# The second MLP product of two more chunks by seven block products, and a new order for every engine

## The chip, the cores and the metric

The kernel runs on one core of a Trainium2 chip. The core has five engines, each with a queue of its own that it works off in order: PE (TensorE, matrix products), DVE (VectorE), ACT (ScalarE), POOL (GpSimd) and SP (SyncE, here only issuing DMAs). DMAs are also issued from the queues of POOL and ACT. An instruction that waits holds up everything behind it in its queue. The metric is the device time of one execution in microseconds (us).

## The reference

Two stages follow each other. The first is attention over 4 batches, 8 heads, 768 positions and 64 features, in which a query sees the 8 first keys and the 96 last ones:

```python
scores = scale * np.matmul(q, k.transpose(0, 1, 3, 2)) + bias
a = softmax(np.where(is_global | is_local, scores, -1e9))
x = np.matmul(a, v)                      # heads side by side: 4 x 768 x 512
```

The second takes the real part of a two-dimensional Fourier transform of x, adds x, normalises and applies an MLP of width 2048:

```python
u = x + np.real(fft(fft(x, axis=1), axis=2))
un = (u - mean(u)) / np.sqrt(var(u) + 1e-6)
out = u + np.maximum(un @ w_ch1, 0.0) @ w_ch2
```

## The kernel before

**Stages.** The four batches go one after the other through attention (functions `trans`, `score`, `av`), the transform (`fold_0` for batch 0 and `fold_s`, `fold_d` for the others on DVE, `y_unit` and `u_unit` on PE) and the MLP. The work of different batches overlaps: while the MLP of one batch fills PE, the attention and transform of the next are put between its products. The MLP works on 12 chunks of 256 rows, three to a batch, each made of two tiles of 128 rows.

**First product.** `ph_unit(c, jp)` makes two of the 16 blocks of 128 hidden features of chunk c: eight matmuls of 256 columns into a bank `ph` (there are two such banks), then the ReLU on ACT (line 1383) or DVE (line 1384) into the tile `hT` of the chunk. Two chunks' hidden values have a place at a time, so chunk 2 can start when chunk 0's second product is done. Chunks 9 to 11 make the first product by seven block products (class `Seven`, line 1471), which is not touched.

**Second product, plain form.** Chunks 0 and 1 (all c below `CS = 2`) use `pg_unit`: for each of the two row tiles, four parts of four matmuls of 512 columns (line 1583), each part needing one quarter of W2 and two `ph` units. DVE then takes the bank, multiplies by the reciprocal deviation of the row (made on POOL, lines 1329 and 1330, token `rstd`) and adds u (line 1594); a DMA stores the result.

**Second product, seven block products.** The other chunks use `s_sums` and `pg_units`. The hidden values of a chunk are four blocks A(t, half), by row tile and by half of the hidden features; W2 is four blocks B(half, column half). With sums of A blocks (S1 to S4, four DVE instructions of 128x1024, lines 1661 to 1674) and sums of B blocks (made once), seven products of a 128x1024 by a 1024x256 block do the work of eight. The units are p1, p45 (two products), p6, p7 and p32 (two products), on line 1697; each product is eight matmuls of 256 columns. After each unit DVE evicts the bank and adds to u (line 1715): 256 columns for p1 and p6, 512 for the others.

**Sums of W2.** `w2_sums(i)`, for the two halves i of the blocks, has two pieces: `one` (token `w2a`, line 1633) makes B11-B01 in the tile `misc`, which until then holds the tables of the masks for the scores of batches 0 and 1; `rest` (token `w2t`, lines 1637 to 1639) makes three more, one of them in place, over a block of W2 itself. As `pg_unit` reads that block, `rest` has to wait until the eight last parts of chunks 0 and 1 are done (token `pgdone`). Two of the sums lie in the tile `tt`, which holds queries and keys of batch 1 first and then the rows x of batch 1; `rest` waits for those to be read.

**Order.** A planner (class `Plan`) emits the instructions; the order on each engine is written out in `ORDER`, as a list of names for each of the five queues. A letter names the stream: A for attention, M for the transform ("mixing"), H for the first product, G for the second; `T` is everything made at set-up. `G4.0` is the first piece of other engines' work that follows PE unit `G4`. A name stands in the list of the engine that does it, so that the list also says whether ACT or DVE makes a ReLU or a copy. Before, G0 to G15 are the parts of chunks 0 and 1, and G16 to G20 are p1, p45, p6, p7 and p32 of chunk 2. The eight quarters of W1 and W2 are loaded by DMAs from POOL (lines 1888 and 1893).

Of the kernel before, what the change touches and what calls it, by code (L numbers as in the profile page):

```python
# [12 lines left out]
ALU = mybir.AluOpType  # L13
# [11 lines left out]
class Plan:  # L25
# [132 lines left out]
            if ring.n == 0:  # L158
                self.rings[ring].append((ring.e, ring.k))

    SHARED = {"kB": 1, "vB": 1, "sid": 1, "f1": 0, "f2": 0, "f3": 0, "z": 0, "g0": 0, "w": 0, "s": 0, "su": 0, "w2a": 0, "w2t": 0, "ex": 0}
    SLOW = ((0.56, 1.0, 1.0), (0.38, 0.7, 1.0))
    COPIES = ("vB", "kB")
    ports = ()
# [75 lines left out]
    def unit_start(self, unit):  # L240
# [7 lines left out]
        if not there:  # L248
# [11 lines left out]
    EARLY = ("qk2", "qk1", "v0", "v2", "qk3", "v1", "v3")  # L260
    ORDER = {
# [10 lines left out]
        ),  # L272
        "ACT": (
# [10 lines left out]
        ),  # L284
        "DVE": (
# [13 lines left out]
        ),  # L299
        "POOL": (  # L300
# [5 lines left out]
        ),  # L306
        "SP": (
            "T.6 T.0 T.9 T.127 T.35 T.133 T.10 T.128 G7.1 T.91 T.134 T.136 G3.1 T.137 T.130 T.100 T.131 T.101 T.176 T.182 T.102 T.177 T.185 T.34 T.206 "
            "T.183 T.140 T.186 T.212 T.205 T.211 T.179 T.149 T.180 T.263 T.150 T.151 T.222 T.223 T.228 T.189 T.229 T.198 T.199 T.200 T.245 T.239 T.240 "
            "T.246 T.258 T.256 T.257 "  # L310
        ),
    }

# [61 lines left out]
def dve2(n):  # L375
    return 0.075 + n / 1920.0
# [7 lines left out]
def kernel(  # L384
# [22 lines left out]
    FB = 2  # L407
    DM = ()
    PEF = (1, 3)
    CS = 2  # L410
    NTD = 3
    assert (B, H, S, Dh, NG, NL) == (4, 8, 768, 64, 8, 96)

# [1214 lines left out]
    def w2_sums(i):  # L1628
        k0 = slice(4 * i, 4 * i + 4)
        k1 = slice(NK + 4 * i, NK + 4 * i + 4)  # L1630

        def one():
            VT(W2T(1)[:, k0], W2[0][:, k1, HC:Dm], W2[0][:, k0, HC:Dm], op=ALU.subtract)

        def rest():
            w = W2[0]
            VT(W2T(3)[:, k0], w[:, k0, HC:Dm], w[:, k0, 0:HC], op=ALU.subtract)
            VT(W2T(0)[:, k0], w[:, k1, HC:Dm], W2T(3)[:, k0], op=ALU.subtract)
            VT(W2T(2)[:, k0], w[:, k1, 0:HC], W2T(0)[:, k0], op=ALU.subtract)
        pl.later([("DVE", dve2(1024), one)], [("w2", 3), ("w2", 1)] + [("ex", 1, hp, g) for hp in range(HP) for g in range(3)], 0.0, [("w2a", i)], rank=2)  # L1640
        pl.later([("DVE", 3 * dve2(1024), rest)], [("w2a", i), ("pgdone",)] + free("tt", WTI), 0.0, [("w2t", i)], rank=2)

    def s_sums(c):
        hs = [("h", c, jp) for jp in range(NJ // 2)]
# [43 lines left out]
    def pg_units(c):  # L1688
# [99 lines left out]

        h0 = [("h", c, jp) for jp in range(4)]
        h1 = [("h", c, jp) for jp in range(4, 8)]  # L1790
        ws = [("w2t", 0), ("w2t", 1)]
        wd = [("w2", a) for a in range(4)]
        PG.append((h0 + wd + [("D",)], ("pg", "ph") if c >= NP * B - 2 else ("pg",), p1))
        PG.append((h1 + [("s", c, 1)] + ws, ("pg", "ph") if c >= NP * B - 2 else ("pg",), p45))
        PG.append(([("s", c, 2), ("ra", c, 0)] + ws, None, p6))
        if lean:
            PG.append(([("s", c, 3), ("ra", c, 1), ("w2a", 0), ("w2a", 1)], None, p7))
# [213 lines left out]
```

## Time and profile before

| | |
|---|---|
| runs shown | 243.38, 244.39, 245.47 us; median 244.39 |
| profiled execution | 244.25 us, span of its instructions 242.4 us |
| granted TensorE clock | 1.000 |
| busy in the span: PE, weight loads | 230.6 us, 188.2 us |
| busy: DVE, ACT, POOL | 206.4, 143.3, 115.7 us |
| HBM read, written | 31.44 MB, 8.65 MB |

How to read the rows of the profile that follow: "L1697" is line 1697 of the kernel; a group's row has line, engine, operation, output <- input, the shape, the count, then "busy us, mean ns of one" and the idle time of the engine just before it. "PE pgD L1697 <- DVE tt L1639: 1.1, 1, 1.1" among the waits says that PE was idle 1.1 us in total, once, for 1.1 us at most, before line 1697, until DVE's line 1639 had written `tt`. A chain piece such as "59.23 1.73 PE pg L1583 x8" has start, length, engine, tile, line and count. In a row of a stretch of time ("24.20:50.20") stand its length, then the busy time of PE, of its weight loads (PEld), of DVE, ACT and POOL, each with its count of instructions, the granted clock, the DMA share and the GB/s.

### The profile page before, as it was taken

The page shows a single profiled execution, that of the slowest core. Times are in us where ns is not written, and L with a number is a line of the kernel's source. Part 1 is how long each engine was busy: PE and PEld are TensorE (multiplying, and loading weights), DVE is VectorE, ACT ScalarE, POOL GpSimd, SP SyncE. Part 2 cuts the span into 40 slices and gives each one's busy share as a digit, 9 for nine tenths or more (in the row PEclk, how much of TensorE's full clock was granted, in tenths as well). Part 3 has the DMA queues.
Part 4 walks back from the last instruction along what each step waited for, and adds up shares of the span by engine and source line. Part 5 has one row for each costly group of instructions (what it writes and reads, how often), then busy time and mean ns, then how long its engine had stood idle before and what let it go on. Part 6 is the DMA issues. An engine that isn't in the chain of part 4 may idle for free.

```text
span 242.4 us, 7226 instructions
## 1 busy us (share of the span) xinstructions
PE 230.6 (95%) x3026; PEld 188.2 (78%) x3026; DVE 206.4 (85%) x463; ACT 143.3 (59%) x233; POOL 115.7 (48%) x161
## 2 busy tenths in 40 slices
PE   7898899899999999889999999999999999999993
PEld 3465677598677668678988888898889899888882
DVE  3478997979961898999999899999998899988992
ACT  2288469974127978665268848845754588376300
POOL 8998769975800319999029854104140350003020
PEclk9999999999999999999999999999999999999999
DMA  7999999999999998999999956964892363103003
GB/s 181 166 164 180 203 209 193 206 207 168 129 159 178 206 182 66 136 178 96 133 220 294 200 76 192 177 32 87 252 271 46 78 141 66 25 0 143 34 26 147
DMA packets 103248, 35.44 MB, mean 146 GB/s; under 512 B 91088, under 2 KB 98640, under 8 KB 103216
## 3 DMA queue, kind: packets, MB, share of 16 engines
q0 software_dynamic: 72448, 19.16, 78.1%
q1 hardware_dynamic: 27216, 13.08, 25.6%
q10 hardware_dynamic: 3552, 2.75, 4.6%
q8 instruction: 23, 0.38, 0.6%
q14 instruction: 9, 0.07, 0.1%
HBM read 31.44 MB, written 8.65 MB: 165 GB/s over the span
## 4 chain that ended last, share of the span: by engine, by line
PE 77%; DVE 12%; ACT 4%; DMA 3%; issue 2%; POOL 1%; DVEq 0%; SPq 0%; POOLq 0%
PE ph L1378 22%; PE pgD L1697 14%; PE pgA L1697 10%; PE phA L1471 4%; PE py L1139 4%; PE pav L856 4%; PE pg L1583 4%; PE phX L1471 3%; DMA qkT<-qk 3%; ACT ex L800 3%; PE pu L1226 3%; PE pz L1860 2%; DVE x L868 2%; DVE ex L812 2%; PE sc L771 2%
## 5 line engine op out<-in xcount | busy, mean ns | idle before, releaser
L1378 PE MATMUL ph<-unT,w 128*128 128x256 f16 x576 | 71.4, 273 | 0.0
L1378 PEld LDWEIGHTS <-w 128*128 128x128 f16 x576 | 55.2, 98 | 8.4
L1383 ACT ACTIVATE hT<-ph 128x512 f16<-128x512 f32 x63 | 36.9, 596 | 41.7 <-PE ph L1378 41.4
L1697 PEld LDWEIGHTS <-hT 128*128 128x128 f16 x288 | 27.8, 98 | 4.8 <-issue 1.4
L797 ACT ACTIVATE er<-sc 128x1024 f16<-128x1024 f32 (+1 forms) x24 | 22.2, 951 | 10.0 <-DVE ex L812 6.0
L800 ACT ACTIVATE ex<-sc 128x1024 f16<-128x1024 f32 (+1 forms) x24 | 21.4, 959 | 8.5 <-PE sc L739 8.5
L1329 POOL TENSOR_SCALAR sm<-sm 128x2 f32<-128x2 f32 x12 | 5.2, 432 | 42.2 <-ACT un L1322 41.6
L1568 POOL DMA_INDIRECT out_dram<-u,back x4 | 5.4, 1345 | 30.7 <-DVE u L1715 30.4
L569 POOL DMA_DIRECT2D qk<-in_k_dram x16 | 13.5, 845 | 12.6 <-DMA qkT<-qk 8.4
L1715 DVE SCALAR_TENSOR_TENSOR u<-pgA,sm,u 128x256 f32<-128x256 f32 (+1 forms) x30 | 16.9, 565 | 1.5 <-PE pgA L1697 1.4
L1715 DVE SCALAR_TENSOR_TENSOR u<-pgD,sm,u 128x512 f32<-128x512 f32 (+1 forms) x21 | 15.0, 719 | 2.6 <-PE pgD L1697 2.5
L812 DVE TENSOR_TENSOR ex<-er,mk 128x1024 f16<-128x1024 f16 (+1 forms) x24 | 16.1, 688 | 0.0
L1583 PE MATMUL pg<-w,hT 128*128 128x512 f16 x64 | 15.5, 379 | 0.0
L1322 ACT ACTIVATE un<-un 128x512 f16<-128x512 f16 x24 | 15.0, 629 | 0.5 <-DMA unT<-un 0.5
L856 PE MATMUL pav<-v,ex 128*128 128x65 f16 x224 | 13.1, 193 | 1.9 <-DVE x L868 1.1
L856 PEld LDWEIGHTS <-ex 128*128 128x128 f16 x352 | 12.7, 97 | 2.8 <-issue 1.1
L569 POOL DMA_DIRECT2D qk<-in_q_dram x16 | 13.9, 879 | 0.0
L1152 ACT ACTIVATE zy<-py 128x1024 f16<-128x1024 f32 (+1 forms) x13 | 10.7, 825 | 4.3 <-PE py L1139 4.2
L868 DVE TENSOR_TENSOR x<-pav,rc 128x384 f16<-128x384 f32 x24 | 12.6, 554 | 0.6
L1384 DVE TENSOR_SCALAR hT<-ph 128x512 f16<-128x512 f32 x9 | 6.2, 685 | 7.1 <-PE ph L1378 7.0
L624 ACT ACTIVATE qk<-phA 128x512 f32<-128x512 f32 x12 | 6.9, 595 | 7.8 <-PE phA L1471 7.8
L1139 PE MATMUL py<-t,ww 128*128 128x256 f16 x80 | 11.2, 273 | 0.0
(217 smaller groups left out, 563.8 us busy)
## 6 DMA issues: line engine op xcount, KB each, us to landing
w<-in_moe_w_ch_dram POOLq DMA_DIRECT2D x8, 512.0 KB, 11.4
out_dram<-u SPq DMA_DIRECT2D x15, 256.0 KB, 3.5
v<-in_v_dram POOLq DMA_DIRECT2D x16, 192.0 KB, 7.0
qk<-in_k_dram POOLq DMA_DIRECT2D x16, 96.0 KB, 4.9
qk<-in_q_dram POOLq DMA_DIRECT2D x16, 96.0 KB, 5.0
xr<-xd SPq DMA_DIRECT2D x3, 512.0 KB, 4.0
xd<-x ACTq DMA_DIRECT2D x2, 768.0 KB, 5.3
ex<-w POOLq DMA_DIRECT2D x3, 512.0 KB, 6.7
```

Source lines behind the costliest of these rows:

```text
L569: nc.gpsimd.dma_start(qk16[n][:, w, :, h], src[b, h0 + h].rearrange("(i m) d -> m i d", m=P))
L797: A(mine(), cut(pa), AF.Exp, 0.0, 0.125)
L800: A(cut(expst[hp][:, :, g * 512:g * 512 + (384 if g == 2 else 512)]), cut(pa), AF.Exp, 0.0, 0.125)
L812: VT(o, mine(), m, op=ALU.mult)
L856: nc.tensor.matmul(o[:, s * 65:(s + 1) * 65], lhsT, w, start=(a == 0), stop=(a == len(ops) - 1), skip_group_check=True)
L868: VT(X[b][:, 3 * (k.start + h):3 * (k.start + h) + 3, 2 * hp * Dh:(2 * hp + 2) * Dh].rearrange("p y (h d) -> p y h d", d=Dh), pv[:, h, :, ...
L1139: nc.tensor.matmul(o, lhsT, rhs, start=(x == 0), stop=(x == len(ops) - 1))
L1378: nc.tensor.matmul(ph[:, a * CH:(a + 1) * CH].rearrange("p (x m) -> p x m", x=2), W1[0][:, d, jb * P:(jb + 1) * P], UNT[c][:, :, d, :], st ...
L1383: pl.later([("ACT", act(512), lambda: A(dst, ph, AF.Relu)), ("DVE", dve(512), lambda: V.tensor_scalar_max(dst, ph, 0.0))], [], e, [("h", c ...
L1583: nc.tensor.matmul(pg, HT[c][:, jb, t * P:(t + 1) * P], W2[0][:, jb, :], start=(jb == 0), stop=(jb == NJ - 1))
L1697: nc.tensor.matmul(o, lhs(j), rhs(j), start=(first and j == 0), stop=(j == NK - 1), skip_group_check=True)
L1715: V.scalar_tensor_tensor(o, x, r(t), acc, op0=ALU.mult, op1=ALU.add)
```

## The change

- `CS` goes from 2 to 0: chunks 0 and 1 also make their second product by `s_sums` and `pg_units`, and `pg_unit` is no longer used. No one waits for `pgdone`.
- With `CS = 0` the rows x of batch 1 lie where those of batch 0 lay (tile `x`) and no longer in `tt`; the sums of W2 in `tt` wait for the queries and keys only.
- `w2_sums` gets three pieces: `one` (one instruction), `middle` (two, token `w2b`) and `rest` (one, the sum in place). They make the same four sums in the same eight instructions. `one` of half i now names the two quarters of W2 that it reads (i and 2 + i) instead of quarters 1 and 3; p6 needs `middle`, p45 also `rest`.
- The lists of all five engines are new.

In the new lists G0 to G4 are p1, p45, p6, p7, p32 of chunk 0, G5 to G9 of chunk 1, and so on; T.270 to T.275 are the pieces of `w2_sums` (`one`, `middle`, `rest` of half 0, then of half 1); T.201 to T.204 and T.207 to T.210 are S1, S2, S4, S3 of chunks 0 and 1. Thirty pieces of work that DVE did go to ACT and one to POOL; eight that ACT did and four that POOL did go to DVE. Of these, in the stretch from about 24 to 50 us: the copies of the turned queries and keys of pairs 5 to 7 (`A26.1`, `A30.1`, `A34.1`), the copy of batch 0's rows `M5.0`, a scaling copy `M0.1`, the copy of chunk 0's turned rows `M10.0` and two evictions of the transform (`M3.0`, `M8.1`) go from DVE to ACT; four such evictions (`M0.0`, `M2.1`, `M3.1`, `M8.0`) go from ACT to DVE, and key copies `A25.0`, `A26.0`, `A30.0` from POOL to DVE.

The diff, with the lists cut to the parts of PE and DVE in which chunks 0 and 1 have their second product:

```diff
-    SHARED = {..., "w2a": 0, "w2t": 0, "ex": 0}
+    SHARED = {..., "w2a": 0, "w2b": 0, "w2t": 0, "ex": 0}
...
         "PE": (
...
-            "A28 M2 M3 M8 A39 A32 M7 A33 A31 A40 M6 A27 M9 M10 M12 A41 H2 H3 A44 H5 H4 A42 H1 A43 H6 M11 H0 H7 M13 G4 G0 H13 G5 G6 H9 H14 G1 G7 G2 H8 "
-            "M18 G3 H15 M15 H11 H10 G8 H16 H18 G12 H12 M14 H17 H20 A47 A46 G9 G13 M16 A51 G14 G10 H19 A53 H21 G11 A45 G15 M17 H23 H22 G16 H30 A52 A54 "
+            "A39 M3 A28 A32 M9 M7 A29 A40 M6 A27 M12 A33 A41 A31 M10 A43 H6 A42 H0 A44 H7 H3 M11 H4 H2 H1 H12 H15 H11 H5 H8 H10 G0 H14 H13 M13 G1 H9 G2 "
+            "M14 M15 G3 M18 G4 G5 H16 H19 A46 A47 H17 H20 A53 A51 G7 G6 A45 M16 G8 H21 H18 M17 H23 G10 H22 G9 A56 A54 H24 A57 H29 H31 A52 H26 G12 A48 "
...
         "DVE": (
...
-            "M7.11 M10.0 M7.12 M7.10 M12.0 M12.2 A41.0 M7.13 A44.0 A42.0 A43.0 M12.4 M12.5 T.93 H7.0 T.94 T.95 T.96 T.97 T.98 M13.0 H14.0 H15.0 G7.0 "
-            "G3.0 H12.0 M14.0 H17.0 T.123 T.261 T.259 A47.1 M16.0 H20.0 M16.2 A46.1 M16.6 A51.1 A53.1 G11.0 G15.0 T.260 T.201 T.262 A45.1 T.202 G16.0 "
+            "M12.0 M12.2 M7.11 A41.0 A43.0 T.273 A42.0 A44.0 T.274 T.93 T.275 T.94 T.95 T.270 T.96 T.271 T.272 T.201 T.97 T.202 G0.0 T.98 G2.0 T.204 "
+            "T.203 G1.0 G3.0 T.207 M18.0 T.208 G4.0 G5.0 A46.1 T.210 A47.1 H17.0 H20.0 G7.0 A53.1 A51.1 G6.0 M16.0 G8.0 M16.2 T.209 A45.1 M16.6 T.123 "
...
-    CS = 2
+    CS = 0
...
         def one():
             VT(W2T(1)[:, k0], W2[0][:, k1, HC:Dm], W2[0][:, k0, HC:Dm], op=ALU.subtract)
 
+        def middle():
+            VT(W2T(0)[:, k0], W2[0][:, k0, 0:HC], W2T(1)[:, k0], op=ALU.add)
+            VT(W2T(2)[:, k0], W2[0][:, k1, 0:HC], W2T(0)[:, k0], op=ALU.subtract)
+
         def rest():
-            w = W2[0]
-            VT(W2T(3)[:, k0], w[:, k0, HC:Dm], w[:, k0, 0:HC], op=ALU.subtract)
-            VT(W2T(0)[:, k0], w[:, k1, HC:Dm], W2T(3)[:, k0], op=ALU.subtract)
-            VT(W2T(2)[:, k0], w[:, k1, 0:HC], W2T(0)[:, k0], op=ALU.subtract)
-        pl.later([("DVE", dve2(1024), one)], [("w2", 3), ("w2", 1)] + [("ex", 1, hp, g) for hp in range(HP) for g in range(3)], 0.0, [("w2a", i)], rank=2)
-        pl.later([("DVE", 3 * dve2(1024), rest)], [("w2a", i), ("pgdone",)] + free("tt", WTI), 0.0, [("w2t", i)], rank=2)
+            VT(W2T(3)[:, k0], W2[0][:, k0, HC:Dm], W2[0][:, k0, 0:HC], op=ALU.subtract)
+        pl.later([("DVE", dve2(1024), one)], [("w2", i), ("w2", 2 + i)] + [("ex", 1, hp, g) for hp in range(HP) for g in range(3)], 0.0, [("w2a", i)], rank=2)
+        pl.later([("DVE", 2 * dve2(1024), middle)], [("w2a", i)] + free("tt", WTI), 0.0, [("w2b", i)], rank=2)
+        pl.later([("DVE", dve2(1024), rest)], [("w2a", i), ("pgdone",)], 0.0, [("w2t", i)], rank=2)
...
-        ws = [("w2t", 0), ("w2t", 1)]
+        ws = [("w2b", 0), ("w2b", 1)]
+        wt = [("w2t", 0), ("w2t", 1)]
...
-        PG.append((h1 + [("s", c, 1)] + ws, ("pg", "ph") if c >= NP * B - 2 else ("pg",), p45))
+        PG.append((h1 + [("s", c, 1)] + ws + wt, ("pg", "ph") if c >= NP * B - 2 else ("pg",), p45))
```

More of the change, by code (lines that the diff above doesn't have):

```diff
@@ L159, in op_go @@
                 self.rings[ring].append((ring.e, ring.k))
-    SHARED = {"kB": 1, "vB": 1, "sid": 1, "f1": 0, "f2": 0, "f3": 0, "z": 0, "g0": 0, "w": 0, "s": 0, "su": 0, "w2a": 0, "w2t": 0, "ex": 0}
+    SHARED = {"kB": 1, "vB": 1, "sid": 1, "f1": 0, "f2": 0, "f3": 0, "z": 0, "g0": 0, "w": 0, "s": 0, "su": 0, "w2a": 0, "w2b": 0, "w2t": 0, "ex": 0}
     SLOW = ((0.56, 1.0, 1.0), (0.38, 0.7, 1.0))
@@ L262 @@
         "PE": (
[9 rows of a table removed]
[8 rows of a table added]
         ),
         "ACT": (
[10 rows of a table removed]
[11 rows of a table added]
         ),
         "DVE": (
[13 rows of a table removed]
[13 rows of a table added]
         ),
         "POOL": (
[5 rows of a table removed]
[5 rows of a table added]
         ),
         "SP": (
-            "T.6 T.0 T.9 T.127 T.35 T.133 T.10 T.128 G7.1 T.91 T.134 T.136 G3.1 T.137 T.130 T.100 T.131 T.101 T.176 T.182 T.102 T.177 T.185 T.34 T.206 "
-            "T.183 T.140 T.186 T.212 T.205 T.211 T.179 T.149 T.180 T.263 T.150 T.151 T.222 T.223 T.228 T.189 T.229 T.198 T.199 T.200 T.245 T.239 T.240 "
-            "T.246 T.258 T.256 T.257 "
+            "T.6 T.0 T.9 T.127 T.35 T.10 T.133 T.128 T.134 T.206 T.136 T.91 T.130 T.137 T.205 T.100 T.131 T.101 T.176 T.177 T.185 T.182 T.102 T.216 T.34 "
+            "T.217 T.140 T.186 T.223 T.183 T.222 T.179 T.149 T.180 T.276 T.150 T.151 T.189 T.233 T.234 T.240 T.239 T.198 T.199 T.200 T.257 T.250 T.256 "
+            "T.251 T.269 T.267 T.268 "
         ),
```

66 rows, old and new, of the table ORDER are left out of this document.

## The prediction

> **What bounds the kernel now.** I read the page's shares and slices first, then the chain of waits, then the stretches of time in which the change acts.
>
> ```profile
> span 242.4 us, 7226 instructions
> ...
> PE 230.6 (95%) x3026; PEld 188.2 (78%) x3026; DVE 206.4 (85%) x463; ACT 143.3 (59%) x233; POOL 115.7 (48%) x161
> PE   7898899899999999889999999999999999999993
> DVE  3478997979961898999999899999998899988992
> ACT  2288469974127978665268848845754588376300
> PE 77%; DVE 12%; ACT 4%; DMA 3%; issue 2%; POOL 1%; DVEq 0%; SPq 0%; POOLq 0%
> ```
>
> PE is busy in nearly every slice and carries 77% of the chain that ended last. DVE is full almost as often, but has a hole in slices 12 and 13 (67 to 79 us). ACT is the engine with room, except in slices 7 and 8.
>
> ```profile
> 24.20:50.20 26.00, 24.00 (x430) 17.68 (x427) 23.32 (x71) 19.25 (x27) 22.14 (x36) 1.00 1.61 203
> 49.90:63.70 13.80, 13.80 (x168) 11.14 (x167) 12.11 (x29) 6.26 (x12) 9.40 (x14) 1.00 1.91 175
> 90.00:110.00 20.00, 18.21 (x282) 15.49 (x281) 18.91 (x33) 13.34 (x22) 19.08 (x27) 1.00 1.47 130
> 110.00:190.00 80.00, 80.00 (x1072) 70.72 (x1071) 74.99 (x159) 49.99 (x79) 30.46 (x36) 1.00 0.88 156
> ```
>
> The columns are length, then PE, weight loads, DVE, ACT and POOL busy. From 50 us on PE stands still only between 90 and 110 (1.79 us); from 110 to 190 it is busy 80.00 of 80. So PE work taken away after 50 us comes off the end, and a new wait of PE is added to it, one for one. The time before 50 us counts too, since everything after it starts from there.
>
> Where the 1.79 us come from, the chain in order of time and the list of waits show:
>
> ```profile
> 81.65 7.38 DMA qkT<-qk
> 89.55 0.83 POOL qk L569
> 90.82 0.72 POOL sm L1330
> 92.23 0.74 DVE u L1594
> 93.71 1.01 DVE tt L1638
> ```
>
> ```profile
> PE pgD L1697 <- DVE tt L1639: 1.1, 1, 1.1
> PE pav L856 <- DVE ex L812: 0.6, 1, 0.6
> PE ptu L1351 <- ACT un L1313: 0.8, 1, 0.8
> PE sc L739 <- POOL mk L712: 0.6, 1, 0.6
> ```
>
> POOL's queue stands behind a load whose buffer is freed by a slow transposing DMA; chunk 1's `rstd` is behind that load, chunk 1's evictions (L1594) behind `rstd`, and the late sums of W2 (L1637 to L1639) behind the evictions in DVE's queue. p45 of chunk 2 then waits 1.1 us for `tt`, and DVE, in arrears, makes PE wait another 0.6 us for a mask product.
>
> **PE's part of the change.** The pieces of the chain give the prices on PE:
>
> ```profile
> 48.66 0.69 PE pav L856 x22
> 55.72 0.87 PE ph L1378 x8
> 56.59 0.45 PE ptu L1351 x8
> 59.23 1.73 PE pg L1583 x8
> 111.86 0.56 PE sc L771 x20
> 117.36 0.87 PE pgA L1697 x8
> ```
>
> The plain form costs four times 1.73, 6.92 us a chunk, the seven products 7 x 0.87 = 6.09. Two chunks save 2 x 0.83 = 1.66 us, all after 59 us, where PE is full: -1.66. The form with seven products issues 112 weight loads and matmuls instead of 64; that they keep pace at 0.109 us each is shown by the 0.87 for eight. The Trainium skill says otherwise ("TensorE: Matmul & The Clock Gate", Back-to-back issue gap): in a stream of load and matmul pairs it has about 131 ns for a 512-column matmul, fewer than two of 256 columns could take. By it the plain form would cost 64 x 0.131 = 8.4 us and the change would save no PE time (an estimate from that page). The row for L1583 has 0.216 each, so the trace does not bear the page out here.
>
> **DVE's part around 50 to 77 us.** Two chunks add eight sums of hidden blocks, and four evictions of 256 and six of 512 columns in the place of four of 512 (L1594, 0.74 each above). The eight sums of W2, the last of which were made around 94 us (the chain above), move to between 53 and 67 us.
>
> ```profile
> L1661 DVE TENSOR_TENSOR eg<-hT 128x1024 f16<-128x1024 f16 x6 | 4.5, 754 | 0.0
> L1633 DVE TENSOR_TENSOR misc<-w 128x1024 f16<-128x1024 f16 x2 | 1.3, 670 | 0.0
> L1638 DVE TENSOR_TENSOR tt<-w 128x1024 f16<-128x1024 f16 x2 | 1.7, 846 | 0.1
> L1715 DVE SCALAR_TENSOR_TENSOR u<-pgA,sm,u 128x256 f32<-128x256 f32 x20 | 9.4, 476 | 1.2 <-PE pgA L1697 1.2
> L1715 DVE SCALAR_TENSOR_TENSOR u<-pgD,sm,u 128x512 f32<-128x512 f32 x19 | 14.1, 744 | 1.5 <-PE pgD L1697 1.3
> L1315 DVE TENSOR_SCALAR un<-u,sm 128x512 f16<-128x512 f32 x17 | 8.5, 507 | 0.1
> L1384 DVE TENSOR_SCALAR hT<-ph 128x512 f16<-128x512 f32 x9 | 6.2, 685 | 7.1 <-PE ph L1378 7.0
> ```
>
> New work on DVE is 8 x 0.754 + 4 x 0.476 + 2 x 0.744 = 9.4 us. Its cover is what leaves DVE for ACT (eight ReLU evictions at 0.685, five `un` at 0.507 and more) and the hole after 67 us. The tightest point is p45 of chunk 0, which needs S1 of chunk 0 and all sums of W2. DVE does from 49.9 us (the first normalisation of batch 1) what the row 49.90:63.70 holds, 12.11 us, less three `un` (1.52) and one ReLU (0.69) that now go to ACT, which is 9.9; then the eight sums of W2, at between 0.67 and 0.85 each, 5.4 to 6.8, of which I take 6.0 as L1633 and L1638 stand on both sides of it; then S1, 0.75. So S1 is there at 49.9 + 16.65 = 66.6 us if DVE never waits. PE, from the first `av` of batch 1 at 48.66, has four `av` (2.76), fifteen `ph` (13.05), p1 (0.87), three turnings (1.35) and one score that the new order puts later (0.56) ahead of p45: 67.2 us. PE comes 0.6 us after S1. In the stretch of before, DVE waited 13.80 - 12.11 = 1.7 us; if it waits as long again, p45 starts 1.1 us late, and with the dearer sums 1.9. The units behind p45 on PE (p6, the `y` units, p7, p32) and then chunk 2's first product, whose hidden buffer p32 frees, all wait with it. I take +0.5, with 0 to 3.4 as bounds: the 3.4 is that wait of 1.7 us and all nine sums at the 1.01 us of the chain's piece of L1638 (2.3 more), less PE's 0.6.
>
> With the sums of W2 early, p45 of chunk 2 finds them ready: -1.1. The 0.6 us wait for the mask product came from the arrears: -0.6. What is late next is the chunk's own S sum, one instruction.
>
> **The stretch to 50 us.**
>
> ```profile
> L707 ACT ACTIVATE qkT<-pt 128x1536 f16<-128x1536 f16 x1 | 1.4, 1450 | 0.2 <-PE pt L680 0.2
> L1208 ACT ACTIVATE u<-px 128x1024 f32<-128x1024 f32 x2 | 2.1, 1030 | 0.0
> L1358 ACT ACTIVATE unT<-ptu 128x1024 f16<-128x1024 f16 x1 | 1.0, 1019 | 0.0
> L1054 DVE TENSOR_SCALAR zy<-pf 128x256 f16<-128x256 f32 x2 | 0.9, 441 | 0.5 <-ACT zy L1052 0.5
> L1152 ACT ACTIVATE zy<-py 128x512 f16<-128x512 f32 x6 | 3.6, 596 | 2.4 <-PE py L1139 2.4
> ```
>
> ACT takes on three copies of turned queries and keys (3 x 1.45), `M5.0` (1.03), `M10.0` (1.02), `M0.1` (0.44, DVE's price) and two evictions, and loses four (net -2 x 0.596): +5.65. It has 19.25 us there, so 24.9 of 26.0. DVE gets shorter by the same copies, less three key copies from POOL, whose handing over cost PE the 0.6 us of L712. The order puts chunk 0's `un` and turned rows at the end of this list, and the first `ph` needs them. For the copies to cost nothing ACT must stay nearly without idle time. I take +0.5; the bounds are -1.4 (the waits for L712 and L1313 go) and +5.65 (ACT idles as long as before).
>
> **What costs nothing, and its cover.** The rows of batch 1 at batch 0's place have to wait for the last reader of batch 0's rows, which is the unit M6 on PE; it stands ahead of the first `av` of batch 1 in the old list and the new. Quarters of W2 are now loaded ahead of three of W1:
>
> ```profile
> L1893 POOL DMA_DIRECT2D w<-in_moe_w_ch_dram x4: 745/761/787, 35.8 to 46.0; - x4
> DMA to landing us min/median/max: 9.2/13.2/15.8
> ```
>
> The last quarter lands at 61.8 us at the latest by these; p1 and the second set of sums need all four at some 62 to 64 us. If that cover is gone, each microsecond is PE's. On POOL chunk 1's `rstd` now stands ahead of the load that held it. On SP a store of chunk 0 stands ahead of a transpose and the read of batch 1's rows, and waits for p7's eviction at some 74 us; their users come past 85 us.
>
> A new order can bring waits anywhere later, where the old one had none from 110 to 190. I take +0.8, about half of what the stretch 90 to 110 lost, with 0 to 1.8 as bounds.
>
> **Sum:** -1.66 - 1.1 - 0.6 + 0.5 + 0.5 + 0.8 = -1.56. Against the profiled execution, 244.25 us (a span of 242.4 and 1.85 around it), that gives 242.7. The median of the runs, 244.39, is 0.14 above it, less than the runs scatter, so I leave 242.7.
>
> **Rivals.**
> - *A better start.* DVE was the fuller engine up to 50 us (23.32 against 19.25); relieved, both PE waits there go (-1.4), and the new order has no waits of its own: -1.66 - 1.7 - 1.4 + 0.5 = -4.3, 240.0 us. For it speaks that the copies leave the busier engine; against it, how full ACT gets.
> - *DVE becomes the bound from 50 to 77.* p45 starts 3.4 us late, and nothing later takes that up, as PE has no idle time to give: -1.56 + 2.9 = +1.3, 245.6 us. For: both arrive within 0.6 us. Against: DVE had waits and a hole, and in the new order most of its inputs are old.
> - *ACT holds up the first product.* Its 6.75 us of idle time up to 50 us are waits for PE and DVE that stay; the turned rows of chunk 0 come 5.65 us late and all of PE after them: -1.56 - 0.5 + 5.65 = +3.6, 247.8 us. It decides from 3.2 us of idle time kept in the stretch on, with which the late start (24.9 + 3.2 - 26.0 = 2.1) eats the gain of 2.06 of all else. For: slices 7 and 8 are ACT's fullest now. Against: most of its idle time was waiting for products whose inputs DVE made.
> - *The smaller matmuls do not keep pace*, and PE saves nothing: -1.56 + 1.66 = +0.1, 244.4 us. The 56 matmuls of L1697 in each of ten chunks speak against it.
>
> **Numbers.** Forecast 0.48, better start 0.14, DVE 0.21, ACT 0.14, pace 0.03. A difference of 1% (2.4 us) is about what can be told from none here. Faster by more than that means under 241.95 us: all of the better start and, as the forecast's 242.7 lies 0.75 above that line and its terms are good to 1.5, 0.20 of its 0.48: 0.34. Slower means over 246.8: ACT, and a little of DVE's upper end, 0.16. Within 1%: 0.50. The range goes from 240.1 to 246.9, which leaves out one tenth at each end.
>
> **What would show it.** Right: no rows of L1583 and 112 more matmuls on L1697 at 0.87 us for eight; the sums of W2 between 53 and 67 us; no wait of pgD for `tt`; PE busy without break from the first `ph`. Wrong: a wait of pgD for DVE around 67 us over 1 us (DVE's bound); the first `ph` later than 50.5 us with ACT's `unT` or `un` as what it waited for; waits of PE past 110 us in sum over 2 us.

## The result, and the profile after

The kernel after takes 243.07 us (median; 242.28 to 245.22), the kernel before, on the same chip, 244.69. The ratio is 0.994, with a 95% interval of 0.9916 to 0.9964: about 1.5 us or 0.6% less, where 242.7 was forecast and 244.39 was the median before. That lies within the 1% that the prediction took as the least it could tell from none; in this group of runs the interval leaves out 1 all the same. In each group a few executions of a kernel take some per cent longer than the rest, or more, whatever its lists: the medians given for the groups take them in, the ratios leave them out.

The profiled execution of after is the longest of the 19 in its group, 245.22 us (a span of 243.4). Two further profiles of the same kernel took 244.44 us and 241.93 us (a span of 240.1). The longest and the shortest are shown, since the difference between them turned out to be the most instructive part. First, the page of the kernel after:

```profile
span 243.4 us, 7339 instructions
...
PE 231.1 (95%) x3074; PEld 193.7 (80%) x3074; DVE 201.5 (83%) x461; ACT 158.3 (65%) x255; POOL 111.9 (46%) x155
PE   7699899989999996999999999999999999999992
...
DVE  3357896989996888489999898999896899898992
ACT  2299599997868855682456877643957677377400
...
PEclk9999999999999998899999999999999999999998
```

PE has 48 matmuls more (112 of the seven products less 64 of the plain form). Its busy time of 231.1 us is above the 230.6 of before, but at a granted clock of 0.990 in the mean. The execution of 241.93 us has 1.000, as the profile of before has, and there it is 2.3 us less than before:

```profile
PE 228.3 (95%) x3074; PEld 192.2 (80%) x3074; DVE 203.7 (85%) x461; ACT 157.9 (66%) x255; POOL 111.6 (46%) x155
```

DVE's hole between 67 and 79 us is filled (its slices 12 and 13 were 6 and 1 and are 9 and 6), and ACT has 15 us more. In the longest execution PE's slice 16 (91 to 97 us) is a 6, and the granted clock dips there and in the next one. The same in the stretches that the prediction used, for the longest execution:

```profile
24.20:50.20 26.00, 24.05 (x433) 17.10 (x431) 21.95 (x72) 22.80 (x27) 19.10 (x29) 1.00 1.58 206
49.90:63.70 13.80, 13.71 (x176) 12.41 (x176) 12.96 (x27) 11.56 (x26) 10.24 (x13) 1.00 1.92 174
90.00:110.00 20.00, 18.14 (x302) 15.17 (x301) 14.92 (x39) 13.69 (x23) 17.45 (x24) 0.91 1.74 145
110.00:190.00 80.00, 79.92 (x1036) 70.32 (x1035) 73.12 (x154) 48.26 (x77) 26.81 (x34) 1.00 0.93 154
```

and for the one of 241.93 us:

```profile
24.20:50.20 26.00, 23.64 (x427) 16.86 (x427) 21.45 (x72) 22.37 (x26) 18.79 (x28) 1.00 1.59 208
90.00:110.00 20.00, 19.65 (x348) 16.92 (x346) 18.21 (x45) 13.48 (x23) 19.22 (x26) 1.00 1.73 139
110.00:190.00 80.00, 79.91 (x1021) 70.21 (x1019) 72.53 (x154) 50.49 (x82) 25.85 (x35) 1.00 0.92 155
```

ACT is busy for 22.4 to 22.8 of the first 26.0 us, where 24.9 was forecast. From 110 to 190 PE still waits for less than 0.1 us. Between 90 and 110 it stands still for 1.86 us in the one execution, with a mean clock of 0.91, and for 0.35 us in the other. Before, it was 1.79 us.

The waits of PE in the longest execution:

```profile
PE ph L1378 <- DMA unT<-un: 1.8, 1, 1.8
PE pz L1863 <- DVE eg L1857: 1.4, 1, 1.4
PE sc L739 <- DVE qkT L704: 1.2, 1, 1.2
PE pav L856 <- DVE x L868: 0.9, 1, 0.9
PE pt L680 <- ACT hT L624: 0.8, 1, 0.8
PE ptu L1351 <- ACT un L1313: 0.5, 1, 0.5
```

The wait of pgD for `tt` (1.1 us) and that of an `av` for the mask product of DVE's line 812 (0.6) are gone, as forecast. A new wait heads the list: the first product of chunk 3 waits for its turned rows. The chain there, in order of time:

```profile
84.83 0.89 PE pgA L1699 x8
...
85.75 1.32 DVE u L1276 x4
...
87.30 0.72 ACT un L1313
...
88.39 6.41 DMA unT<-un
...
94.85 1.42 PE ph L1378 x8
```

The transposing DMA is issued at 88.39 and lands 6.4 us later. In the execution of 241.93 us it is issued at 87.72 and takes 5.46, and `ph` starts at 93.23.

### The profile page after: what moved, and what is told of

It reads as the page before. It is cut to its first block, busy times and chain, and to the rows that moved or that the text cites. A ratio compares the mean times of both kernels' runs of the same rounds, so it can differ in the third digit from the quotient of the medians.

```text
span 243.4 us, 7339 instructions
## 1 busy us (share of the span) xinstructions
PE 231.1 (95%) x3074; PEld 193.7 (80%) x3074; DVE 201.5 (83%) x461; ACT 158.3 (65%) x255; POOL 111.9 (46%) x155
## 4 chain that ended last, share of the span: by engine, by line
PE 81%; ACT 6%; DVE 5%; DMA 5%; issue 1%; ACTq 0%; DVEq 0%
PE ph L1378 23%; PE pgD L1699 16%; PE pgA L1699 12%; PE phA L1471 4%; PE pav L856 4%; PE py L1139 4%; PE phX L1471 3%; PE pu L1226 3%; DMA unT<-un 3%; DMA u<-in_k_dram 3%; ACT ex L800 2%; PE pt L680 2%; PE sc L771 2%; PE sc L739 2%; PE sc L763 2%; PE pf L1047 2%
## 5 line engine op out<-in xcount | busy, mean ns | idle before, releaser
L1383 ACT ACTIVATE hT<-ph 128x512 f16<-128x512 f32 x69 | 40.6, 596 | 30.0 <-PE ph L1378 29.6
L1699 PEld LDWEIGHTS <-hT 128*128 128x128 f16 x352 | 34.0, 98 | 4.0
L1329 POOL TENSOR_SCALAR sm<-sm 128x2 f32<-128x2 f32 x12 | 3.6, 301 | 64.2 <-ACT un L1322 62.3
L1717 DVE SCALAR_TENSOR_TENSOR u<-pgA,sm,u 128x256 f32<-128x256 f32 (+1 forms) x36 | 20.4, 566 | 2.5 <-PE pgA L1699 1.9
L1717 DVE SCALAR_TENSOR_TENSOR u<-pgD,sm,u 128x512 f32<-128x512 f32 (+1 forms) x25 | 18.0, 724 | 4.9 <-PE pgD L1699 4.6
L868 DVE TENSOR_TENSOR x<-pav,rc 128x384 f16<-128x384 f32 x32 | 16.7, 553 | 0.7
L921 POOL DMA_INDIRECT xr<-xd,back x3 | 3.5, 1151 | 22.9 <-DVE ex L812 11.7
L1699 PEld LDWEIGHTS <-sb 128*128 128x128 f16 x128 | 12.2, 98 | 1.7
L827 POOL COPY vB<-v 128x528 f16<-128x528 f16 x14 | 9.5, 681 | 5.6 <-DMA v<-in_v_dram 4.6
L1699 PE MATMUL pgD<-tt,hT 128*128 128x256 f16 x88 | 11.4, 273 | 0.0
```

Source lines behind the costliest of these rows:

```text
L868: VT(X[b][:, 3 * (k.start + h):3 * (k.start + h) + 3, 2 * hp * Dh:(2 * hp + 2) * Dh].rearrange("p y (h d) -> p y h d", d=Dh), pv[:, h, :, ...
L1383: pl.later([("ACT", act(512), lambda: A(dst, ph, AF.Relu)), ("DVE", dve(512), lambda: V.tensor_scalar_max(dst, ph, 0.0))], [], e, [("h", c ...
L1699: nc.tensor.matmul(o, lhs(j), rhs(j), start=(first and j == 0), stop=(j == NK - 1), skip_group_check=True)
L1717: V.scalar_tensor_tensor(o, x, r(t), acc, op0=ALU.mult, op1=ALU.add)
```

## The experiments

The medians below are of runs in three groups, each on one chip with the kernel before beside it: 244.16, 245.4 and 244.6 us for the kernel before. The same kernel's median differs by some 0.2 us (after, once in each of three groups: 243.07, 242.84, 242.96) to 1.7 us (before, run twice in one group: 245.4 and 243.7), so differences under half a microsecond are not read as such, and those between groups are read with care.

### What PE's saved time is worth

The kernel after, with the first of the seven products of chunks 0 and 1 made twice over (twice 0.87 us on PE, nothing else), beside the kernel after unchanged:

```diff
-            prod(A_[:, 0:HC], a(0, 0), bw(0, 0), True)
+            for _ in range(2 if c < 2 else 1):
+                prod(A_[:, 0:HC], a(0, 0), bw(0, 0), True)
```

> The changed kernel once more, for a profile of an ordinary execution. PE theory: the gain of 1.6 us over before comes again (ratio about 0.994), and the wait of the first product of chunk 3 for its transposing DMA near 93 us, 1.85 us in the first profile, is there again with 1 us or more. Rival (that wait was an accident of the one slow execution): it is under 0.5 us here.

> The changed kernel, in which p1 of chunks 0 and 1 is computed twice over (the second time starts the bank anew): 16 matmuls more, 2 x 0.87 = 1.74 us of PE. PE theory: each microsecond of PE work between 60 and 80 us is one of the whole, +1.7 us against the changed kernel. Rival, DVE bounds that stretch or a transfer behind it: PE has slack there and the time rises by less than 0.9 us.

Measured: after 242.84 us, with the doubled product 243.98: 1.14 us for 1.74 us of PE, two thirds. Samples drawn again from the executions of both put this difference between 0.8 and 1.8 us, so neither the 1.7 of the theory nor the rival's bound of 0.9 is excluded. Where the rest would go, the list of waits suggests: with the doubled product there is no wait for chunk 3's turned rows, since PE arrives later; in the profile of after made beside it this wait is 0.4 us. At two thirds, the 1.66 us that chunks 0 and 1 save would be worth about 1.1 us.

The gain itself did not come again in full. The ratio to before was 0.9976 (0.9949 to 1.0004) in this group and 0.9963 (0.993 to 0.9996) in the third, about 0.6 and 0.9 us where the first group has 1.5. The wait of chunk 3, forecast with 1 us or more, was 0.4 us in the profile of this group; long ones came again with two other lists (1.7 us with `first_ph`, 1.6 with `early_old2`, both below).

### Half of the new order

Two kernels with half of the new order each. `early_old` has the order before up to the first products (about 50 us) and the order after from there; `early_new` is the kernel before with the new order up to there.

> The changed kernel with the old order and the old sharing between engines up to the first product of attention and values of batch 1 (about 50 us); everything after it as changed. My sum put +0.5 us on the new early part: this run would be 0.5 us faster than the changed kernel. Rival, a better start: the new early part gains 1.4 us, and this run is 1.4 us slower. Rival, ACT holds up the first product: this run is 3 us faster or more.

> The kernel before with the new order and sharing up to the first product of attention and values of batch 1, plain form for chunks 0 and 1 as before, everything after it as before. My sum: +0.5 us against before. Rival, a better start: -1.4 us. Rival, ACT holds up the first product: +3 us or more. If the two halves add up, the step from this run to the changed kernel is what the seven products and the later order bring, -2.06 us by my sum.

Measured: `early_old` 248.31 us (ratio 1.0204, 1.0158 to 1.025), `early_new` 246.53 us (1.0136, 1.0087 to 1.0185). Both halves alone are slower than both whole orders, so neither value is a price of its half. For `early_new`, which came out 2.4 us above before where +0.5 was forecast, the cause stays open. Its one profile is of an execution of 252.06 us, 5.5 us above its median; the first `ph` starts at 51.70 us there and has waited 0.5 us for ACT's `unT`. By itself this run would speak for the rival in which ACT holds up the first product. For `early_old` the list of waits shows where the time goes. DVE, then PE:

```profile
DVE misc L1636 <- issue: 5.1, 1, 5.1
...
PE ptu L1354 <- DVE x L871: 4.4, 1, 4.4
```

The lines are shifted by three: L1636 here is L1633 after, the first sum of W2. In the old order of POOL's loads the quarters of W2 come late: POOL issues them at 37.39, 39.59, 41.01 and 47.61 us. DVE reaches the sum at 54 us and waits until 59.17, and behind it in DVE's queue stand the rows of batch 1, for which PE waits. The row names no releaser ("issue"), so that the missing piece is a quarter of W2 was still to be tested.

The next kernel has the old order up to 50 us on PE, DVE, ACT and SP again, and the new one on POOL, so that two of the quarters of W2 go out from 32.65 us on (in the kernel after from 29.20). In POOL's list, where `A15.0`, `A30.0`, `A25.0` and `A26.0` are key copies that the old order has there, and `T.66` is a copy of values that it has on DVE:

```diff
-"POOL": "T.12 ... T.31 T.66 T.23 T.33 T.32 T.60 ... T.28 T.27 ... T.55 T.56 T.114 ..."
+"POOL": "T.12 ... T.31 T.23 T.33 T.32 A15.0 T.60 ... T.28 A30.0 T.27 ... T.55 A25.0 T.56 A26.0 T.114 ..."
```

> As early_old (order before up to the first products, order after from there), but with GpSimd's loads in the new order, so that the quarters of W2 come as early as after; ScalarE's, VectorE's and TensorE's lists are those of early_old. Theory (the late W2 quarter and the 5.1 us that VectorE waited for it were the cost of early_old): the 4 to 5 us come back, 243 to 244.2 us, near the kernel after, which would show the new division of work between ScalarE and VectorE as worth little either way. Rival (the seam between two orders, or the old division of work, was the cost): 245.5 us or more, and VectorE no longer waits at the first W2 sum.

> early_old2 once more: the order before up to the first products, with the loads of W2 at their new, early places, and the order after from there. Its median of 242.27 us was of six executions. Theory (the new division of work between ScalarE and VectorE up to 50 us costs some 0.5 us, as forecast): again lower than the kernel after, by 0.3 to 0.9 us. Rival (it costs nothing): within 0.2 us of it.

Measured: 242.27 us in a group in which the kernel after was not run, and in the next group 242.85 us, beside 242.96 for the kernel after. DVE's 5.1 us are gone, and more came back than the 4 to 5 us forecast. So the early loads of W2 are a necessary part of the change: left out, they cost more than 5 us. The other part of the new front (the order up to 50 us), the pieces that moved between ACT, DVE and POOL, is worth nothing that these medians can tell. Nor did the first run's gain of the old front (242.27) repeat.

### Does the first product come later

> The kernel before once more, unchanged, for a second profile of it. In the three profiles of the order after, the first MLP product (the first ph) starts at 50.74, 51.38 and 53.22 us; in the one profile of before it starts at 49.18. Theory (the new front, with more work on ScalarE, holds the first product up by 1.5 us or more): ph again near 49.2 (48.7 to 50). Rival (the start of a run moves by itself, with when the first loads land): ph as far out as 51 to 53 here too, and the later start after is no cost of the change. In either case the time is that of the kernel before, ratio 1.00, and the stretch from the first ph to the last matmul near 189 us.

> The kernel after, with two moves in the front: ScalarE writes chunk 0's two un before the exponentials A33 and A31 rather than after A33, and the copy of the turned rows (M10.0, 1.02 us on ScalarE) goes to VectorE (0.68 in the profile before), ahead of the division A41. Theory (ScalarE's chain ex, un, ex, unT sets the first ph): ph about 1 us earlier, and the time 0.4 to 1.0 us lower. Rival (TensorE's total and not its start is what counts, a later start being made up afterwards by work that is otherwise waited for): ph earlier, the time within 0.2 us of the kernel after. It also loses if the division A41 is then late for TensorE.

The second edit, on the lists of ACT and DVE:

```diff
-"ACT": "... M6.0 A27.0 A33.0 M7.5 M7.4 A31.0 M10.0 M7.6 ..."
+"ACT": "... M6.0 A27.0 M7.5 M7.4 A33.0 A31.0 M7.6 ..."
-"DVE": "... M7.11 A41.0 A43.0 ..."
+"DVE": "... M7.11 M10.0 A41.0 A43.0 ..."
```

Measured: the kernel before ran at 243.7 us, ratio 0.9968 (0.9928 to 1.0009) to itself, and in its second profile (of an execution of 248.8 us, 5 us above the median, so it weighs little) the first `ph` starts at 50.89 us, not at 49.18. The three profiles with the old division of work and early loads have it at 52.37, 50.93 and 49.85. The kernel with the moves ran at 243.28; its first `ph` starts at 50.20. The chain before the first `ph` in the kernel after (241.93 us) is ACT's, as feared:

```profile
46.71 0.81 ACT ex L800
47.52 1.22 ACT un L1313 x2
48.74 0.78 ACT ex L800
...
49.55 1.03 ACT unT L1358
...
50.62 1.03 PE ph L1378 x8
```

But the start of the first `ph` moves between executions of one list (49.85 to 52.37 with the old division of work, 50.62 to 53.22 after) by more than the lists differ. Much of that goes with the granted clock of the first 25 us. The profiles of after with the earliest and the latest first `ph`, 50.62 and 53.22 us:

```profile
0.00:25.00 25.00, 19.76 (x318) 11.99 (x319) 14.58 (x43) 15.89 (x18) 23.49 (x36) 1.00 1.87 172
0.00:25.00 25.00, 20.24 (x272) 11.74 (x274) 11.21 (x33) 12.77 (x15) 21.77 (x33) 0.86 1.88 172
```

The profiles with the clock at 1.00 up to 50 us can be compared. In them the first `ph` starts at 50.51 to 50.74 us with the front of after, at 50.20 with the two moves, at 49.85 with the old division of work, and at 49.18 before. Between 49.18 and 49.85 us lies one `av` that PE's later list has ahead of the first `ph` (0.67 us in the chain of after). From there to after, 0.7 to 0.9 us, it is the division of work, and ACT's fuller list is what the chain shows. The starts at 49.18, 49.85 and 50.20 are of one profile each. In the medians none of this shows: making the chain shorter did not make the kernel faster (243.28), and the old division of work gave 242.85 beside 242.96.

### How much margin DVE has

The kernel after with 1.36 us more on DVE ahead of the sums of chunk 0 (the first column difference of W2 three times):

```diff
-            VT(W2T(1)[:, k0], W2[0][:, k1, HC:Dm], W2[0][:, k0, HC:Dm], op=ALU.subtract)
+            for _ in range(3 if i == 0 else 1):
+                VT(W2T(1)[:, k0], W2[0][:, k1, HC:Dm], W2[0][:, k0, HC:Dm], op=ALU.subtract)
```

> The kernel after, with the first column difference of W2 written three times where it was written once: 2 x 0.68 = 1.36 us more on VectorE ahead of the sums of chunk 0, TensorE's work untouched. The profile after has VectorE's operands of chunk 0's second product p45 ready 1.5 us before TensorE gets there. Theory (VectorE has that margin, TensorE stays the bound): no change, 0 to +0.3 us. Rival of the prediction (VectorE is the bound from 50 to 77): all of it shows, +1.2 to +1.4 us, and TensorE waits at p45[0] for VectorE's eg.

Measured: 243.04 us, as the kernel after in the other groups (242.84 and 242.96; it was not run in this one). The timeline of the kernel after around p45 of chunk 0 (start, length, engine and line; profile of 245.22 us):

```profile
64.91 0.69 DVE L1663 TENSOR_TENSOR eg<-hT 128x1024 f16<-128x1024 f16 x1
...
67.00 1.04 PE L1699 MATMUL pgD<-tt,hT 128*128 128x256 f16 x8
...
67.87 1.04 PE L1699 MATMUL pgD<-w,eg 128*128 128x256 f16 x8
```

and of the kernel with the added sums:

```profile
66.43 0.69 DVE L1664 TENSOR_TENSOR eg<-hT 128x1024 f16<-128x1024 f16 x1
66.77 1.04 PE L1700 MATMUL pgD<-tt,hT 128*128 128x256 f16 x8
...
67.64 1.04 PE L1700 MATMUL pgD<-w,eg 128*128 128x256 f16 x8
...
69.70 0.10 PEld L1700 LDWEIGHTS <-sb 128*128 128x128 f16 x1 [0.42 <-DVE sb L1670]
```

Two waits of PE in this profile that the three profiles of after do not have:

```profile
PE sc L771 <- DVE u L1292: 1.3, 1, 1.3
...
PE pgA L1700 <- DVE u L1718: 0.5, 1, 0.5
```

After, S1 is there at 65.60 us, 1.4 us before PE starts p45 and 2.3 before the product that reads it. With 1.36 us more, PE goes through p45 without a wait for S1. At p6 it stands still for 0.5 us: first its weight load waits 0.42 us for S2, then the product for the eviction of p1's bank (line 1718), which stands behind S2 on DVE. So there is a margin at p45, but about 0.5 of the added 1.36 us reach PE at the next unit. The wait of 1.3 us comes at 141 us; whether the added sums bring it is not known. In the median none of it shows.

### The wait of chunk 3's first product

The kernel after with chunk 3's second `un` ahead of an eviction of chunk 1 on DVE, and an `av` of batch 2 ahead of chunk 3's first product on PE; then the same two moves in `early_old2`:

```diff
-"DVE": "... G6.0 M16.0 G8.0 M16.2 T.209 ..."
+"DVE": "... G6.0 M16.0 M16.2 G8.0 T.209 ..."
-"PE": "... A56 A54 H24 A57 H29 ..."
+"PE": "... A56 A54 A57 H24 H29 ..."
```

> The kernel after once more, unchanged, on the same chip as the next three, as their measure. Theory (the first comparison's 1.5 us hold): 242.6 to 243.4 us. Its medians so far are 243.07 and 242.84; a median outside of that range would say that half a microsecond cannot be told between calls.

> The kernel after, with chunk 3's second un written ahead of the eviction of chunk 1's product p7 on VectorE (0.7 us earlier), and batch 2's av A57 (0.7 us of TensorE) put ahead of chunk 3's first product. Theory (the wait of the first ph of chunk 3 for its turned rows, 1.8, 0.4, 0.5, 1.7 and 1.6 us in five profiles of the new order, is a cost that the new order brought, and the granted clock that falls with the long ones is part of it): the wait is gone or under 0.3 us, and the time 0.4 to 1.2 us lower than the kernel after. Rival (the wait is one run's accident of a slow transfer, and in the other executions there is slack): the same time within 0.2 us.

> early_old2 with the two moves of un_first. Theory (both costs are real and lie in different stretches): the two gains add up, 241.2 to 242.0 us. Rival (each was chance, or the one is hidden behind the other): as old2_again within 0.2 us.

Measured: the kernel after 242.96 us, with the moves 243.06; the combined kernel 242.29 us, beside 242.85 without the moves. In the profile with the moves on the kernel after, no wait for turned rows is left, but two others have come:

```profile
PE sc L773 <- DVE u L1294: 0.8, 1, 0.8
PE pav L858 <- ACT er L799: 0.8, 1, 0.8
```

The `av` put ahead waits for its exponentials. So this experiment exchanged one wait for others of about the same size, and does not say what the wait alone costs. The moves bring nothing that shows. The combined kernel has the lowest median of its group, between its two forecasts, with a ratio of 0.994 (0.9898 to 0.9983); the kernel after has 0.9963 (0.993 to 0.9996) there, and 0.994 in the first group. No version that is better for certain was found.

## Why the prediction was right

**PE's 1.66 us.** The plain form's rows are gone, and in the rows of line 1699 each of the seven operand pairs has 16 matmuls more (profile of 241.93 us; before, these two had 72 and 48, at 272 and 273 ns):

```profile
L1699 PE MATMUL pgA<-w,hT x88: 272/273/283, 63.8 to 223.8; 128*128 128x256 f16 x88
L1699 PE MATMUL pgD<-w,eg x64: 272/273/273, 67.7 to 183.6; 128*128 128x256 f16 x64
```

These durations are not the pace, since one matmul starts before the last has ended (eight of 272 ns make 2.2 us); the pace is in the starts of the two products of p45 above, 67.00 and 67.87 us, again 0.87 us for eight. The saving itself stands in PE's busy time. The two profiles with a mean clock of 1.000, before and the 241.93 us of after, have 742 and 745 matmuls behind them at 50.2 us. From there to the end PE is busy for 186.43 us of 192.20 before and for 184.92 of 189.90 after: 1.5 us less work, and 0.8 us less idle time. These are single profiles, and that of after is of one of its shorter executions. (That PE stands still only between 90 and 110 us leaves out the end: from 190 us on it is idle for 4.0 us before and for 4.4 after.)

Whether each microsecond of it is one at the end, "one for one", stays open: the runs with the doubled product give 0.65 to one, with one to one still possible. The rival of a slower pace falls. So does, for this kernel, the Trainium skill's figure of about 131 ns for a 512-column matmul in a stream of load and matmul pairs ("TensorE: Matmul & The Clock Gate", Back-to-back issue gap), by which this saving would not exist; the row for L1583 has 0.216 us.

**The sums of W2.** They stand between 51.9 and 65.0 us, at 0.68 each, and both waits that the prediction put down to them are gone (-1.7). The forecast set +0.8 against it for waits anywhere in the new order. That wait came, in one place: the first product of chunk 3, with 1.8, 0.4 and 0.3 us in the three profiles of after, or 0.35 to 1.86 us of PE idle between 90 and 110. From 110 to 190 less than 0.1 us came. How much of the 1.7 us is left in the median was not measured by itself: the gain over before was 1.5, 0.6 and 0.9 us in the three groups, and with about 1.1 us of it from PE, all other terms together come to between 0.4 us of gain and 0.5 of loss.

**DVE against PE at p45.** S1 was forecast for 66.6 us and came at 65.6; PE was forecast for 67.2 and came at 67.0. The +0.5 was too much by all of it: p45 waits for nothing, even with 1.36 us more on DVE, though p6 then does. The sum gave DVE 16.65 us of work from 49.9 us on, and in the profile it is busy for 14.86 us of the 15.70 up to 65.6; of the difference, 0.6 us are the eight sums of W2, which take 5.4 us. The rival of DVE as the bound, at 0.21, falls with this.

**The stretch to 50 us.** The forecast had ACT at 24.9 of 26.0 us; it is 22.4 to 22.8, in part because two `un` of line 1322, 1.2 us, have moved out behind 50.2 us. The sign named as wrong came, a first `ph` after 50.5 us behind ACT's `unT`, and at a like clock this start is 0.7 to 0.9 us later than with the old division of work. In the time it is not seen: the old division, with W2 early, gives 242.85 against 242.96 us. The +0.5 was picked between bounds of -1.4 and +5.65, and no row set it; the runs put it at zero, give or take half a microsecond or more, which neither confirms nor refutes it. One thing that the forecast did not look for points its way: from DVE's last instruction to the end of the span it is 4.4 to 4.5 us in all eight profiles with the new front and 3.9 to 4.0 in the six with an old one. What stands in that half microsecond is not known. The rival in which ACT holds up the first product, at +3.6, falls for the changed kernel, while `early_new` stays unexplained. That of a better start falls too: of the two waits that it wanted gone, that for `un` is still there with 0.5 of 0.8 us, and that for line 712, now on DVE, with 0.2 and 0.6 us in two of the three profiles of after.

**What costs nothing.** The early quarters of W2 were costed only as a risk to others. The runs show the other side: without them the kernel takes over 5 us more, as DVE waits for a quarter with the rows of batch 1 behind it.

So the sum came out within 0.4 us of the time and within 0.1 us of the step (-1.56 forecast, 243.07 - 244.69 = -1.62 measured), and PE's term carries it. That it is so close is in part luck: the +0.5 at p45 was not there, that of the first 50 us is open, the gains from the W2 sums were partly eaten by the new wait, and in the two other groups the step was smaller.

## What to carry to other kernels

Where one engine is busy without a break, work taken off it is the term to trust, here, by the medians, at two thirds of its face value; what a new order adds or takes elsewhere was of both signs. A piece moved ahead in one queue has to be followed back to the load that feeds it: here the first sum of W2 at its new place was only free because a load had moved with it. And before a shift of a microsecond in one stage is put down to a change, further profiles of the same lists show how much that stage moves by itself; here those with the same granted clock were the ones to compare.

## What the runs showed of the hardware

Behind a wait of PE the granted clock was sometimes lower, so that the wait cost twice. In the longest execution of after, PE stands still for 1.85 us between 90 and 95 us, and in the five microseconds behind it the granted clock is 0.66:

```profile
90.00:95.00 5.00, 3.15 (x61) 2.52 (x60) 4.86 (x19) 3.43 (x5) 4.84 (x7) 1.00 1.62 124
95.00:100.00 5.00, 5.00 (x60) 4.03 (x63) 3.04 (x7) 1.50 (x3) 3.49 (x6) 0.66 2.64 146
```

That is another 1.7 us lost (0.34 of 5 us); from 50.2 us on, PE is busy for 1.8 us more than in the execution of 241.93 us. In `old2_again`, with the old division of work, PE is idle 1.23 us there, and the clock stays at 1.00:

```profile
90.00:95.00 5.00, 3.77 (x67) 3.08 (x65) 4.13 (x18) 3.27 (x5) 4.84 (x8) 1.00 1.65 138
95.00:100.00 5.00, 5.00 (x80) 4.30 (x78) 3.88 (x9) 3.38 (x8) 4.67 (x6) 1.00 2.53 149
```

With `first_ph` an idle time of 1.75 us was followed by 0.66 as well. In `early_old`, where PE was idle for 3.27 us between 55 and 60, the clock was 0.88 in those five microseconds and 0.50 in the next five. After 1.58 us in `early_old2` it stayed at 1.00. The length alone does not decide it: in the second profile of before PE was idle for 2.00 us between 165 and 170, and the clock stayed at 1.00. That the wait is what lowers the clock was not tested by itself. The longest and the shortest profile of after differ by 3.3 us, and 1.5 us more of idle time between 90 and 110 and 1.7 us of clock make up nearly all of it.

The transposing DMA of the same rows took 6.41 us in one execution and 5.46 in the other, against a median of 3.2 us for all nine of its kind in the first. Issued 0.67 us later and 0.95 us longer, it made PE wait 1.8 us in the one, against 0.3 in the other.
